# An opening list in another order, and another tile for the kept words' differences

## The chip, the core and the metric

The kernel runs on one core of a Trainium2 chip. Its time is that of the device for one execution, in microseconds, the median of several runs. The core has TensorE (PE; its weight loads are shown apart as PEld), VectorE (DVE), ScalarE (ACT), GpSimd (POOL) and SyncE (SP), which here only issues DMAs. Each works through its own instructions in order and waits on semaphores for the others.

## The reference

Attention over a small memory for 8 batches of 8 heads, 576 tokens and 64 dimensions, then a gated MLP from 512 to 1536 and back on all 4608 tokens. Eps terms and the reshaping are left out.

```python
a = softmax(phi, axis=2)                      # phi: batch, head, 576, 32
k_m = einsum('bhsm,bhsd->bhmd', a, k); v_m = einsum('bhsm,bhsd->bhmd', a, v)
attn = softmax(q @ k_m.T / 8)                 # batch, head, 576, 32
x = (attn @ v_m) with the heads side by side  # 4608 x 512
out = (sigmoid(x @ w_gate) * (x @ w_val)) @ w_out
```

The weights arrive as 64-bit floats. The kernel turns them into 32-bit ones itself.

## The kernel before

Batches are numbered 0 to 7. The inner width of 1536 is cut into 12 stripes f of 128, the tokens of a batch into a first part of 256 (c = 0) and a second of 320 (c = 1). The kernel never forms x: it multiplies the memory's v by each stripe's gate and value weights (the tiles u_hi and u_lo) and multiplies that by the attention (at). Most products are made of three with rounded high and low parts; stripes 0 to 2 of batch 0 are plain ones.

The first twelve steps (stripes 0 to 3 of batches 0, 1 and 2) are not written as loops. OPENING is a list of 401 small tasks, and the kernel emits them in that order. A helper (`step`) makes each engine take its instructions in just the order of the list, so the list sets the order on PE, DVE, ACT and POOL, and that of the DMAs on SP. Some tasks: `phi b`, `kvm b g`, `kvt b`, `q b c` and `words f k r` load (words: the 64-bit weights of stripe f; k = 3 is all of its gate and value weights, 0 and 1 their halves, 2 the output weights); `mag f k` (ACT) and `bits f k` (DVE, two or four goes) convert them; `amax`, `aexp`, `asum` are the softmax of phi; each `mem b n` is the next piece of batch b's memory (transposes, copies, products with k and v); `scores`, `blocks`, `smax`, `sub`, `sexp`, `nsum`, `nmul`, `across`, `upper` and `lower` lead to at (upper and lower are its rounded high part and the rest); `u`, `uhi`, `ulo`; `gate`, `sig`, `mul`, `ghi`, `gleft`, `glo` and `out` are the MLP; `leave` takes a finished accumulator away; and `warm n` is n filling products of 256 columns on an identity matrix, whose result nobody reads.

Behind the list the steps 12 to 35 are loops over the other stripes of batches 0 to 2, with later work put beside them. In six of these steps (KEEP_W, step: pair of stripes) a pair of weight stripes is written back to memory for the batches 3 to 7; for the first 64 rows the second half is written as a difference, which DVE makes in a tile:

```python
for j in range(2):
    t = mb.tile([P, DM], F32, name="row", bufs=4)[:D]
    t = t.rearrange("p (k n) -> p k n", k=NKT)
    nc.vector.tensor_tensor(t, w[:D, j, :, :P], w[:D, j, :, P:], op=ALU.subtract)
    move(kept_k[:D, j, :, P:], t)
```

The tile row has four buffers, which the partial sums of the output use too. The tile e has one; it holds the exponentials of a batch's scores.

Of the kernel before, what the change touches and what calls it, by code (L numbers as in the profile page):

```python
# [49 lines left out]
aexp 0 1; mag 0 1; amax 1; mem 0 2; words 1 3 2; mem 0 4; kvt 0; kvm 0 0; aexp 1 0; asum 0; mem 0 5;  # L50
kvm 0 1; mag 1 3; bits 0 0; mem 0 3; mem 0 1; warm 36; mem 0 11; aexp 1 1; warm 16; mem 0 6; bits 1 3;
phi 2; bits 1 3; asum 1; bits 1 3; mem 0 7; bits 0 1; q 0 0; mem 0 8; mem 0 9; bits 1 3; q 0 1;
mem 1 5; scores 0 0; mem 1 3; bits 0 1; amax 2; aexp 2 0; mem 0 10; mem 1 0; scores 0 1; blocks 0 0;
kvm 1 0; smax 0 0; sub 0 0; u 0 1; blocks 0 1; aexp 2 1; mem 1 4; kvt 1; sexp 0 0; nsum 0 0;
words 2 3 2; mem 1 2; mem 2 1; uhi 0 0 1; u 0 0; uhi 0 1 1; mem 1 1; kvm 1 1; words 1 2 3; mem 2 3;
mem 2 4; uhi 0 0 0; smax 0 1; nmul 0 0; sub 0 1; across 0 0; asum 2; uhi 0 1 0; sexp 0 1; mem 1 11;
mag 2 3; warm 9; gate 0 0 0; gate 0 1 0; sig 0 1 0; mem 2 2; nsum 0 1; sig 0 0 0; bits 2 3; nmul 0 1;
bits 2 3; q 1 0; across 0 1; mem 1 6; mul 0 0 0; mag 1 2; words 0 2 2; bits 2 3; mem 1 7; gate 0 0 1;
bits 2 3; nospread; q 1 1; words 3 2 1; sig 0 0 1; mem 1 8; words 3 3 2; kvm 2 1; mag 0 2; mul 0 1 0;
mul 0 0 1; mem 1 10; mem 1 9; u 0 2; scores 1 0; words 2 2 0; uhi 0 0 2; bits 1 2; bits 0 2; uhi 0 1 2;  # L60
blocks 1 0; gate 0 1 1; sig 0 1 1; ghi 0 0 1; scores 1 1; bits 0 2; mag 3 3; mul 0 1 1; kvm 2 0;
bits 1 2; out 0 0 0; blocks 1 1; bits 3 3; smax 1; gate 0 2 0; kvt 2; mag 2 2; mem 2 0; bits 3 3;
sub 1; gate 0 2 1; sig 0 2 1; sexp 1; words 4 2 2; mem 2 5; gleft 0 0 1; upper 0; out 0 0 1; bits 3 3;
mul 0 2 1; ghi 0 1 1; mem 2 6; bits 3 3; ghi 0 2 1; mem 2 11; sig 0 2 0; out 0 1 0; nsum 1; mem 2 7;
u 0 3; nmul 1; mem 2 8; across 1; uhi 0 0 3; uhi 0 1 3; ulo 0 0 3; out 0 1 1; upper 1; lower 0;
ulo 0 1 3; lower 1; q 2 0; q 2 1; mem 2 10; gate 0 3 1; bits 2 2; mul 0 2 0; gleft 0 2 1; kvt 3;
mag 3 2; gate 0 3 0; sig 0 3 1; sig 0 3 0; mem 2 9; bits 2 2; wohi 2; u 1 0 1; mul 0 3 1; mul 0 3 0;
bits 3 2; out 0 2 0; scores 2 0; out 0 2 1; ghi 0 3 0; uhi 1 0 0 1; uhi 1 1 0 1; scores 2 1; bits 3 2;
ulo 1 1 0 1; u 1 2 3; ghi 0 3 1; ulo 1 0 0 1; gleft 0 3 1; wohi 0; wohi 1; blocks 2 0; gate 1 0 1;
wohi 3; glo 0 3 0; sig 1 0 1; uhi 1 0 2 3; blocks 2 1; gate 1 0 0; gate 1 1 0; sig 1 0 0; glo 0 3 1;  # L70
wolo 3; smax 2; out 0 3 1; mul 1 0 1; sub 2; mul 1 0 0; keep 0; ghi 1 0 1; out 0 3 0; uhi 1 1 2 3;
gleft 0 1 1; wolo 0; wolo 1; words 4 3 0; ulo 1 1 2 3; ulo 1 0 2 3; sig 1 1 0; gate 1 3 0; ghi 1 0 0;
gate 1 1 1; gate 1 2 1; glo 1 0 1; wolo 2; sexp 2; phi 3; glo 1 0 0; gleft 1 0 1; mag 4 2; mul 1 1 0;
sig 1 1 1; leave 0 3; ghi 1 1 0; nsum 2; out 1 0 1; leave 0 1; gate 1 2 0; leave 0 0; mul 1 1 1;
gleft 1 1 1; keep 1; leave 0 2; ghi 1 1 1; nmul 2; glo 1 1 0; kvm 3 0; out 1 0 0; glo 1 1 1; sig 1 2 1;
mag 4 3; bits 4 3; u 2 0 1; sig 1 3 0; sig 1 2 0; u 2 2 3; mul 1 3 0; out 1 1 1; ghi 1 3 0;
uhi 2 0 0 1; bits 4 3; bits 4 3; mul 1 2 1; uhi 2 1 0 1; mul 1 2 0; across 2; gleft 1 2 1; ulo 2 0 0 1;
ulo 2 1 0 1; gate 1 3 1; ghi 1 2 1; upper 2; ghi 1 2 0; glo 1 2 1; bits 4 3; lower 2; out 1 2 1;
glo 1 2 0; sig 1 3 1; mul 1 3 1; bits 4 2; ghi 1 3 1; gleft 1 3 1; bits 4 2; words 5 3 0; uhi 2 0 2 3;
gate 2 0 1; amax 3; sig 2 0 1; wohi 4; ulo 2 0 2 3; mag 5 3; glo 1 3 0; mul 2 0 1; out 1 1 0;  # L80
gate 2 0 0; uhi 2 1 2 3; gleft 2 0 1; bits 5 3; sig 2 0 0; out 1 2 0; aexp 3 1; glo 1 3 1; bits 5 3;
words 6 3 1; bits 5 3; ghi 2 0 1; out 1 3 0; mul 2 0 0; bits 5 3; wolo 4; ulo 2 1 2 3; mag 6 3;
out 1 3 1; words 7 3 0; leave 1 3; glo 2 0 1; gate 2 1 0; ghi 2 0 0; gate 2 1 1; leave 1 0; gate 2 3 1;
glo 2 0 0; sig 2 1 0; gate 2 2 0; sig 2 1 1; mul 2 1 0; sig 2 3 1; ghi 2 1 0; leave 1 1; out 2 0 0;
mul 2 1 1; u 0 4 5; mag 7 3; out 2 0 1; leave 1 2; bits 6 3; glo 2 1 0; again 0; gate 2 3 0;
gate 2 2 1; bits 6 3; sig 2 2 0; keep 2; bits 6 3; gleft 2 1 1; aexp 3 0; bits 7 3; mul 2 2 0;
ghi 2 1 1; ghi 2 2 0; uhi 0 0 4 5; bits 7 3; bits 6 3; mul 2 3 1; sig 2 3 0; glo 2 1 1; ghi 2 3 1;
out 2 1 0; gleft 2 3 1; glo 2 2 0; ulo 0 0 4 5; asum 3; sig 2 2 1; bits 7 3; kvm 3 1; mul 2 3 0;
mul 2 2 1; out 2 2 0; uhi 0 1 4 5; words 5 2 2; ghi 2 3 0; glo 2 3 1; ghi 2 2 1; bits 7 3; words 8 0 1;
ulo 0 1 4 5; glo 2 3 0; glo 2 2 1; words 7 2 0; words 6 2 3; gleft 2 2 1; out 2 1 1  # L90
# [1493 lines left out]
```

## Time and profile before

| | us |
|---|---|
| median of 3 runs (lowest, highest) | 717.69 (717.58, 718.09) |
| the profiled execution | 716.45 |
| its span, first to last instruction | 714.7 |
| PE busy | 705.5 |
| DVE busy | 552.8 |
| ACT busy | 446.3 |

Busy time counts instructions that run, not those that wait. Filling products count as busy for PE. In a timeline a bracket behind a row tells how long the engine had been idle before it and what released it.

### The profile page before, as it was taken

The page shows a single profiled execution, that of the slowest core. Times are in us where ns is not written, and L with a number is a line of the kernel's source. Part 1 is how long each engine was busy: PE and PEld are TensorE (multiplying, and loading weights), DVE is VectorE, ACT ScalarE, POOL GpSimd, SP SyncE. Part 2 cuts the span into 40 slices and gives each one's busy share as a digit, 9 for nine tenths or more (in the row PEclk, how much of TensorE's full clock was granted, in tenths as well). Part 3 has the DMA queues.
Part 4 walks back from the last instruction along what each step waited for, and adds up shares of the span by engine and source line. Part 5 has one row for each costly group of instructions (what it writes and reads, how often), then busy time and mean ns, then how long its engine had stood idle before and what let it go on. Part 6 is the DMA issues. An engine that isn't in the chain of part 4 may idle for free.

```text
span 714.7 us, 14239 instructions
## 1 busy us (share of the span) xinstructions
PE 705.5 (99%) x5517; PEld 579.1 (81%) x5517; DVE 552.8 (77%) x1092; ACT 446.3 (62%) x1033; POOL 27.6 (4%) x55
## 2 busy tenths in 40 slices
PE   8999999999999999999999999999999999999997
PEld 7655898888988888888888888887888788788786
DVE  5898998778787775588887779777797777977663
ACT  4755776543354454467877667875777657686553
POOL 0000100111101110100000000000000000000000
PEclk9999999999999999999999999999999999999999
DMA  8966559878956745642176113652323422151102
GB/s 347 406 261 215 209 193 375 283 276 274 320 183 195 277 140 184 249 129 79 60 260 208 60 60 119 225 186 72 107 73 129 146 88 74 61 176 61 60 1 73
DMA packets 36083, 123.21 MB, mean 172 GB/s; under 512 B 3952, under 2 KB 11376, under 8 KB 28848
## 3 DMA queue, kind: packets, MB, share of 16 engines
...
q10 hardware_dynamic: 160, 0.13, 0.1%
...
## 4 chain that ended last, share of the span: by engine, by line
PE 93%; DMA 3%; ACT 1%; DVE 1%; SPq 1%; issue 0%
PE acc L192 39%; PE pu_t L192 20%; PE c L192 11%; PE a L192 9%; PE b L192 7%; PE d L192 7%; DMA kvm<-in_kvm_dram 2%; DMA words<-in_wo_dram 1%; SPq L178 1%; ACT L162 0%; DVE e L499 0%; DVE e L508 0%; ACT sg L167 0%; DVE mx L506 0%; DVE wg L283 0%
## 5 line engine op out<-in xcount | busy, mean ns | idle before, releaser
L192 PE MATMUL acc<-wo_hi,g_hi 128*128 128x512 f32 x372 | 152.2, 409 | 0.0
L192 PE MATMUL acc<-wo_hi,g_lo 128*128 128x512 f32 x372 | 147.1, 395 | 0.0
L192 PE MATMUL acc<-wo_lo,g_hi 128*128 128x512 f32 x372 | 146.7, 394 | 0.0
L192 PE MATMUL pu_t<-at,u_hi 128*128 128x320 f32 (+1 forms) x560 | 116.7, 305 | 0.0
L192 PEld LDWEIGHTS acc<-wo_hi,g_hi 128*128 128x128 f32 x372 | 69.9, 188 | 37.5 <-ACT c_s L1180 16.8
L192 PEld LDWEIGHTS pu_t<-at,u_hi 128*128 128x128 f32 x560 | 92.1, 188 | 8.5 <-issue 2.1
L192 PEld LDWEIGHTS acc<-wo_hi,g_lo 128*128 128x128 f32 x372 | 69.9, 188 | 16.8 <-DVE g_lo L182 0.3
L192 PE MATMUL pu_t<-at,u_lo 128*128 128x256 f32 (+1 forms) x264 | 77.6, 294 | 0.0
L192 PEld LDWEIGHTS acc<-wo_lo,g_hi 128*128 128x128 f32 x372 | 70.1, 188 | 5.7
L1180 ACT COPY c_p<-c 128x288 f32<-128x288 f32 x60 | 23.9, 398 | 67.3 <-PE c L192 66.6
L167 ACT ACTIVATE sg<-pu_t 128x256 f32<-128x256 f32 (+1 forms) x70 | 28.5, 410 | 49.7 <-PE pu_t L192 45.4
L1184 DVE TENSOR_TENSOR z<-c,c_x 128x288 f32<-128x288 f32 x60 | 27.4, 456 | 34.5 <-PE c L192 31.7
L167 ACT ACTIVATE z<-z 128x288 f32<-128x288 f32 x120 | 48.1, 439 | 8.5 <-DVE z L1184 7.6
L1184 DVE TENSOR_TENSOR z<-a,c_s 128x288 f32<-128x288 f32 x60 | 27.2, 453 | 33.1 <-PE a L192 32.4
L192 PEld LDWEIGHTS pu_t<-at,u_lo 128*128 128x128 f32 x264 | 49.6, 188 | 0.0
L698 DVE TENSOR_TENSOR sg<-pu_t,sg 128x320 f32<-128x320 f32 (+1 forms) x69 | 31.1, 454 | 24.0 <-ACT sg L167 14.2
L708 ACT CAST g_hi<-sg 128x256 fp32r<-128x256 f32 x66 | 26.5, 405 | 36.6 <-DVE sg L698 34.6
L1196 ACT CAST g_hi<-z 128x512 fp32r<-128x512 f32 x60 | 37.3, 622 | 10.4 <-DVE z L1191 10.4
L182 DVE TENSOR_TENSOR g_lo<-z,g_hi 128x512 fp32r<-128x512 f32 x60 | 41.0, 683 | 1.6 <-ACT g_hi L1196 1.6
L1191 DVE TENSOR_TENSOR z<-z 128x288 f32<-128x288 f32 x60 | 27.2, 453 | 6.0 <-ACT z L167 1.1
L192 PE MATMUL c<-ring,vT 64*32 64x512 f32 x232 | 31.4, 601 | 0.0
L192 PE MATMUL a<-ring,vT 64*32 64x512 f32 x232 | 31.4, 601 | 0.0
...
## 6 DMA issues: line engine op xcount, KB each, us to landing
...
at<-at SPq DMA_DIRECT2D x18, 576.0 KB, 7.8
q<-in_qT_dram SPq DMA_DIRECT2D x16, 512.0 KB, 5.0
...
words<-in_wo_dram SPq DMA_DIRECT2D x8, 512.0 KB, 9.6
...
```

Of the source, the lines that this page charges most:

```text
L167: last_act[0] = nc.scalar.activation(*args, **kw)
L178: last_move[queue] = queues[queue].dma_start(dst, src)
L182: return nc.vector.tensor_tensor(lo, x, hi.bitcast(F32), op=ALU.subtract)
L192: last_pe[0] = do(*args, **kw)
L698: last_prod[0] = nc.vector.tensor_tensor(prod, ps[1][:, :n], sg[:, :n], op=ALU.mult)
L708: nc.scalar.copy(hi, prod[:, : 2 * P])
L1180: copy(getattr(self, name), self.c if name == "p5" else self.d)
L1184: nc.vector.tensor_tensor(self.z[:, i], x, y, op=ALU.add)
L1191: nc.vector.tensor_tensor(self.z[:, 2 + i], x, self.z[:, i], op=ALU.mult)
L1196: nc.scalar.copy(self.g[0], self.z[:, 2:4, : 2 * P])
```

## The change

The OPENING list is written anew: the same 401 tasks in another order, with other counts of filling products (46, 40, 3 and 2 in place of 52, 36, 16 and 9). The differences of the kept words are made in the tile e instead of two row tiles, and the pair 4 is kept in step 22 instead of 28.

```diff
 OPENING = """
-words 0 0 0; phi 0; mag 0 0; words 0 1 1; table; phi 1; amax 0; aexp 0 0; bits 0 0; warm 52; mem 0 0;
+phi 1; words 0 0 0; phi 0; table; kvt 0; amax 0; aexp 0 0; words 0 1 1; aexp 0 1; warm 46; mem 0 0;
...
-    KEEP_W = {17: 0, 18: 1, 19: 2, 20: 3, 25: 5, 28: 4}
+    KEEP_W = {17: 0, 18: 1, 19: 2, 20: 3, 22: 4, 25: 5}
...
+            diff = att([P, 2 * S], "e")[:D, : 2 * DM].rearrange("p (f k n) -> p f k n", f=2, k=NKT)
             for j in range(2):
-                t = mb.tile([P, DM], F32, name="row", bufs=4)[:D]
-                t = t.rearrange("p (k n) -> p k n", k=NKT)
+                t = diff[:, j]
                 nc.vector.tensor_tensor(t, w[:D, j, :, :P], w[:D, j, :, P:], op=ALU.subtract)
                 move(kept_k[:D, j, :, P:], t)
```

The first loads on SP's queue stood like this before (the weights' words as words_89, or wg for all of stripe 1; phi of batch 0 as ph, that of batch 1 as in_phiT into wg):

```order
L178 DMA words_89<-in_wgv_dram 128x1024
L178 DMA ph<-in_phiT_dram 128x1152
L178 DMA words_89<-in_wgv_dram 128x1024
L178 DMA wg<-in_phiT_dram 128x1152
L178 DMA wg<-in_wgv_dram 128x2048
L178 DMA kvt<-in_kvt_dram 128x512
```

With the change they stand like this:

```order
L179 DMA wg<-in_phiT_dram 128x1152
L179 DMA words_89<-in_wgv_dram 128x1024
L179 DMA ph<-in_phiT_dram 128x1152
L179 DMA kvt<-in_kvt_dram 128x512
L179 DMA words_89<-in_wgv_dram 128x1024
L179 DMA wg<-in_wgv_dram 128x2048
```

The phi of batch 1 has moved to the front, and that of batch 0 from second to third; the six loads are the same.

The first instructions of ACT, before (wg from words is a magnitude, ph from ph an exponential of batch 0's phi, z from ident loads the table, row from pu_t copies transposes):

```order
L265 ACT_TABLE_LOAD
L265 ACTIVATE wg<-words_89 128x512
L167 ACTIVATE z<-ident 128x1
L167 ACTIVATE ph,z<-ph,nmx 128x576 x2
L265 ACTIVATE wg<-words_89 128x512
L413 COPY row<-pu_t 128x512
```

and with the change:

```order
L168 ACT_TABLE_LOAD
L168 ACTIVATE z<-ident 128x1
L168 ACTIVATE ph,z<-ph,nmx 128x576 x2
L266 ACTIVATE wg<-words_89 128x512 x2
L414 COPY row<-pu_t 128x512
```

The first magnitude has moved behind the two exponentials.

The third place is on DVE, from the conversion of stripe 3 (wg) to lower 0 (at from at, batch 0) and lower 1 (at from q, batch 1); sg and g_hi from pu_t are products of the gate, zs the sums of the scores' exponentials e. Before:

```order
L278 SCALAR_TENSOR_TENSOR wg<-wg 128x1024
L698 TENSOR_TENSOR sg<-pu_t,sg 128x320
L283 SCALAR_TENSOR_TENSOR wg<-wg 128x1024
L521 TENSOR_REDUCE zs<-e 128x36
L522 TENSOR_SCALAR zs<-zs 128x36
L523 RECIPROCAL zs<-zs 128x36
L527 TENSOR_TENSOR e<-e,zs 128x1152
L561 STREAM_TRANSPOSE q<-e 128x1152
L182 TENSOR_TENSOR u_lo<-pu_t,u_hi 128x256
L182 TENSOR_TENSOR at<-at 128x1152
```

With the change:

```order
L279 SCALAR_TENSOR_TENSOR wg<-wg 128x1024
L699 TENSOR_TENSOR sg<-pu_t,sg 128x320 x2
L284 SCALAR_TENSOR_TENSOR wg<-wg 128x1024
L699 TENSOR_TENSOR g_hi<-pu_t,sg 128x256
L522 TENSOR_REDUCE zs<-e 128x36
L523 TENSOR_SCALAR zs<-zs 128x36
L524 RECIPROCAL zs<-zs 128x36
L528 TENSOR_TENSOR e<-e,zs 128x1152
L183 TENSOR_TENSOR u_lo<-pu_t,u_hi 128x256
L562 STREAM_TRANSPOSE q<-e 128x1152
L183 TENSOR_TENSOR at<-at 128x1152
```

The product of gate 0 2 0 (g_hi) has come in ahead of the sums (one of the two sg stood further up before), and u_lo stands ahead of the transpose.

## Rows read from the trace of the kernel before

**Rows 1.** The page, part 1: busy time and share of each engine.
```profile
PE 705.5 (99%) x5517; PEld 579.1 (81%) x5517; DVE 552.8 (77%) x1092; ACT 446.3 (62%) x1033; POOL 27.6 (4%) x55
```

**Rows 2.** Windows: stretch, length, busy PE, PEld, DVE, ACT, POOL, clock, DMA, GB/s.
```profile
0.00:60.00 60.00, 54.70 (x631) 38.51 (x632) 48.05 (x82) 36.62 (x77) 0.69 (x6) 1.00 0.77 302
60.00:700.00 640.00, 640.00 (x4827) 531.36 (x4826) 500.22 (x1003) 404.26 (x945) 26.87 (x49) 1.00 0.47 162
```

**Rows 3.** Timeline of PE in the opening: start, length, instruction, idle before.
```profile
1.36 7.97 PE L192 MATMUL acc<-ident 128*128 128x256 bf16 x52 [1.36 <-POOL ident masks.py:199]
...
10.15 4.09 PE L192 MATMUL acc<-ident 128*128 128x256 bf16 x36
...
18.71 1.08 PE L192 MATMUL pu_t<-kvm,row 128*32 128x128 f32 x32 [0.42 <-DMA kvm<-in_kvm_dram]
...
29.24 1.10 PE L192 MATMUL acc<-at,u_hi 128*128 128x256 f32 x4 [0.35 <-DVE at L564]
```

**Rows 4.** Issue on SP (timeline), and us to landing (DMA view), of two loads.
```profile
1.66 0.43 SPq L178 DMA_DIRECT2D words<-in_wgv_dram  x1
2.13 0.54 SPq L178 DMA_DIRECT2D wg<-in_phiT_dram  x1
...
words<-in_wgv_dram SPq DMA_DIRECT2D x1, 512.0 KB, 6.3
...
wg<-in_phiT_dram SPq DMA_DIRECT2D x1, 576.0 KB, 7.2
```

**Rows 5.** Timeline of DVE and ACT from 6 to 23 us.
```profile
6.67 1.41 DVE L372 TENSOR_REDUCE nmx<-ph 128x1 f32<-128x576 f32 x2 [5.53 <-DMA ph<-in_phiT_dram]
...
8.00 0.42 DVE L271 TENSOR_SCALAR wg<-wg 128x512 f32<-128x512 f32 x1
...
9.04 0.67 ACT L265 ACTIVATE wg<-words 128x512 f32<-128x512 f32 x1
...
22.62 0.45 DVE L499 STREAM_TRANSPOSE e<-acc 128x256 f32<-128x256 f32 x1 [1.16 <-PE pu_t L192]
```

**Rows 6.** Windows in the opening, columns as in rows 2.
```profile
0.00:5.00 5.00, 3.64 (x18) 2.52 (x19) 0.27 (x1) 1.28 (x1) 0.69 (x6) 1.00 0.58 169
5.00:10.00 5.00, 5.00 (x44) 4.43 (x43) 2.73 (x5) 3.15 (x8) 0.00 (x0) 1.00 1.03 424
...
8.00:21.46 13.46, 11.55 (x160) 9.71 (x158) 11.01 (x19) 6.80 (x17) 0.00 (x0) 1.00 1.02 416
22.62:57.63 35.01, 33.00 (x400) 21.11 (x399) 33.09 (x57) 25.15 (x55) 0.00 (x0) 1.00 0.72 284
...
29.24:57.91 28.67, 27.01 (x274) 17.01 (x275) 26.89 (x45) 20.15 (x41) 0.00 (x0) 1.00 0.64 252
```

**Rows 7.** Timeline from 34 to 60 us: DVE's waits, lower 0, PE's load.
```profile
34.15 0.42 DVE L698 TENSOR_TENSOR g_hi<-acc,sg 128x256 f32<-128x256 f32 x1 [0.55 <-ACT sg L167]
...
44.02 0.69 DVE L271 TENSOR_SCALAR wg<-wg 128x1024 f32<-128x1024 f32 x1 [0.18 <-ACT wg L265]
...
50.68 1.35 DVE L521 TENSOR_REDUCE zs<-e 128x36 f32<-128x1152 f32 x1 [0.16 <-ACT e L167]
...
55.94 0.42 DVE L182 TENSOR_TENSOR u_lo<-pu_t,u_hi 128x256 fp32r<-128x256 f32 x1 [0.47 <-ACT u_hi L621]
...
56.28 1.35 DVE L182 TENSOR_TENSOR at<-at 128x1152 fp32r<-128x1152 f32 x1
...
57.91 0.19 PEld L192 LDWEIGHTS pu_t<-at,u_hi 128*128 128x128 f32 x1 [0.24 <-DVE at L182]
...
59.94 0.42 DVE L698 TENSOR_TENSOR g_hi<-pu_t,sg 128x256 f32<-128x256 f32 x1
```

**Rows 8.** Timeline of DVE: the longest wait of a kept words' difference.
```profile
190.73 0.68 DVE L1230 TENSOR_TENSOR row<-wg 64x512 f32<-64x512 f32 x1 [4.16 <-DMA part<-row]
```

**Rows 9.** Timeline at gate 2 0 1: its subtraction on DVE, its first products.
```profile
90.47 1.35 DVE L182 TENSOR_TENSOR at<-q,at 128x1152 fp32r<-128x1152 f32 x1
...
92.39 0.46 PE L192 MATMUL pu_t<-at,u_hi 128*128 128x320 f32 x2
```

More of the change, by code (lines that the diff above doesn't have):

```diff
@@ L48 @@
 OPENING = """
-words 0 0 0; phi 0; mag 0 0; words 0 1 1; table; phi 1; amax 0; aexp 0 0; bits 0 0; warm 52; mem 0 0;
[L50 to L90, printed above, removed]
+phi 1; words 0 0 0; phi 0; table; kvt 0; amax 0; aexp 0 0; words 0 1 1; aexp 0 1; warm 46; mem 0 0;
@@ new lines @@
+words 1 3 2; mag 0 0; mag 0 1; kvm 0 0; mem 0 2; mag 1 3; bits 0 1; bits 0 0; mem 0 4; mem 0 5;
+mem 0 3; amax 1; aexp 1 1; asum 0; mem 0 1; bits 1 3; warm 40; mem 0 11; aexp 1 0; bits 0 1; kvm 0 1;
+bits 1 3; warm 3; mem 0 6; phi 2; mem 0 7; bits 0 0; mem 1 5; bits 1 3; mem 0 8; mem 0 9; q 0 0;
+asum 1; bits 1 3; amax 2; q 0 1; mem 1 3; mem 0 10; aexp 2 0; scores 0 0; blocks 0 0; smax 0 0;
+scores 0 1; aexp 2 1; mem 1 0; mem 2 1; u 0 1; sub 0 0; mem 1 4; sexp 0 0; mem 1 2; uhi 0 0 1; mem 1 1;
@@ new lines @@
+blocks 0 1; mem 2 3; kvm 1 0; kvt 1; u 0 0; uhi 0 1 1; words 2 3 2; uhi 0 0 0; mem 1 11; nsum 0 0;
+words 1 2 3; kvm 1 1; smax 0 1; q 1 0; nmul 0 0; mem 2 4; sub 0 1; uhi 0 1 0; sexp 0 1; mag 2 3;
+across 0 0; warm 2; gate 0 1 0; asum 2; nsum 0 1; gate 0 0 0; words 0 2 2; mag 1 2; bits 2 3;
+nmul 0 1; sig 0 1 0; mem 1 6; bits 2 3; across 0 1; mem 2 2; mem 1 7; sig 0 0 0; words 3 2 1; bits 2 3;
+gate 0 0 1; mul 0 1 0; bits 2 3; mem 1 8; sig 0 0 1; mag 0 2; q 1 1; mul 0 0 0; bits 0 2; u 0 2;
+mem 1 10; bits 1 2; mem 1 9; scores 1 0; nospread; uhi 0 0 2; scores 1 1; words 3 3 2; mul 0 0 1;
@@ new lines @@
+gate 0 1 1; kvm 2 0; sig 0 1 1; uhi 0 1 2; blocks 1 0; mag 3 2; bits 0 2; bits 1 2; ghi 0 0 1; upper 0;
+mag 3 3; blocks 1 1; wohi 1; smax 1; out 0 0 0; gate 0 2 1; words 2 2 0; bits 3 3; sub 1; bits 3 3;
+sig 0 2 1; mem 2 0; gate 0 2 0; gleft 0 0 1; bits 3 3; mul 0 2 1; mem 2 5; kvm 2 1; mul 0 1 1;
+sig 0 2 0; out 0 1 0; bits 3 3; out 0 0 1; mul 0 2 0; kvt 2; sexp 1; nsum 1; u 0 3; gleft 0 1 1;
+ghi 0 1 1; nmul 1; mem 2 6; mem 2 11; ghi 0 2 1; uhi 0 0 3; out 0 1 1; uhi 0 1 3; ulo 0 0 3; across 1;
@@ new lines @@
+mem 2 7; mag 2 2; upper 1; lower 0; mem 2 8; ulo 0 1 3; lower 1; bits 2 2; bits 2 2; mem 2 10;
+bits 3 2; wohi 0; gate 0 3 1; gate 0 3 0; gleft 0 2 1; u 1 0 1; q 2 0; mem 2 9; sig 0 3 1; out 0 2 0;
+sig 0 3 0; scores 2 0; uhi 1 0 0 1; q 2 1; keep 0; out 0 2 1; mul 0 3 1; uhi 1 1 0 1; ulo 1 0 0 1;
+bits 3 2; ulo 1 1 0 1; mul 0 3 0; wohi 3; scores 2 1; u 1 2 3; kvm 3 1; blocks 2 0; gleft 0 3 1;
+ghi 0 3 0; gate 1 0 1; glo 0 3 0; wolo 3; kvm 3 0; ghi 0 3 1; blocks 2 1; glo 0 3 1; gate 1 0 0;
+out 0 3 1; uhi 1 0 2 3; smax 2; words 4 3 0; sig 1 0 1; mul 1 0 1; sub 2; wolo 0; ghi 1 0 1; sig 1 0 0;
@@ new lines @@
+uhi 1 1 2 3; sexp 2; mul 1 0 0; gleft 1 0 1; leave 0 2; gate 1 1 1; wohi 2; gate 1 1 0; ulo 1 0 2 3;
+ulo 1 1 2 3; ghi 1 0 0; nsum 2; glo 1 0 1; gate 1 3 0; sig 1 1 1; glo 1 0 0; sig 1 1 0; wolo 1;
+mul 1 1 0; leave 0 3; sig 1 3 0; out 0 3 0; ghi 1 1 0; out 1 0 1; mul 1 1 1; gate 1 2 1; nmul 2;
+ghi 1 1 1; mag 4 3; gleft 1 1 1; gate 1 2 0; leave 0 0; sig 1 2 1; again 0; bits 4 3; out 1 0 0;
+words 4 2 2; leave 0 1; mag 4 2; glo 1 1 0; glo 1 1 1; across 2; bits 4 3; mul 1 2 1; ghi 1 2 1;
+u 2 0 1; sig 1 2 0; uhi 2 0 0 1; keep 1; u 2 2 3; out 1 1 0; wolo 2; phi 3; mul 1 3 0; mul 1 2 0;
@@ new lines @@
+uhi 2 1 0 1; gate 1 3 1; ghi 1 2 0; bits 4 3; ulo 2 0 0 1; glo 1 2 1; upper 2; ulo 2 1 0 1; bits 4 3;
+out 1 1 1; glo 1 2 0; bits 4 2; sig 1 3 1; lower 2; gleft 1 2 1; out 1 2 1; words 5 3 0; uhi 2 0 2 3;
+mul 1 3 1; ulo 2 0 2 3; ghi 1 3 1; gate 2 0 1; bits 4 2; ghi 1 3 0; sig 2 0 1; glo 1 3 0; gate 2 0 0;
+mag 5 3; glo 1 3 1; sig 2 0 0; mul 2 0 1; amax 3; out 1 2 0; mul 2 0 0; kvt 3; bits 5 3; bits 5 3;
+bits 5 3; uhi 2 1 2 3; gate 2 1 0; ghi 2 0 1; gleft 2 0 1; ghi 2 0 0; out 1 3 1; out 1 3 0; glo 2 0 0;
@@ new lines @@
+words 6 3 1; ulo 2 1 2 3; sig 2 1 0; bits 5 3; gleft 1 3 1; mag 6 3; wohi 4; gate 2 3 1; gate 2 2 0;
+bits 6 3; bits 6 3; gate 2 1 1; sig 2 3 1; wolo 4; mul 2 1 0; leave 1 0; words 7 3 0; leave 1 1;
+mul 2 3 1; keep 2; leave 1 3; ghi 2 1 0; glo 2 0 1; sig 2 2 0; sig 2 1 1; out 2 0 0; glo 2 1 0;
+leave 1 2; bits 6 3; mul 2 1 1; u 0 4 5; mul 2 2 0; aexp 3 0; out 2 1 0; ghi 2 2 0; bits 6 3; mag 7 3;
+gleft 2 1 1; glo 2 2 0; gate 2 3 0; gate 2 2 1; bits 7 3; out 2 0 1; uhi 0 0 4 5; ulo 0 0 4 5;
+ghi 2 1 1; glo 2 1 1; words 5 2 2; aexp 3 1; ghi 2 3 1; sig 2 3 0; bits 7 3; words 6 2 3; asum 3;
@@ L91 @@
+bits 7 3; uhi 0 1 4 5; mul 2 3 0; sig 2 2 1; bits 7 3; ghi 2 3 0; mul 2 2 1; glo 2 3 1; ghi 2 2 1;
+words 7 2 0; out 2 2 0; gleft 2 3 1; glo 2 3 0; ulo 0 1 4 5; words 8 0 1; gleft 2 2 1; glo 2 2 1;
+out 2 1 1
 """
```

## The prediction

> **What bounds the kernel now.** I read the busy times of the page first [rows 1]: TensorE (PE) is busy 705.5 of 714.7 us, the next engine 77%. The table of windows then says where the rest is [rows 2]: from 60 to 700 us PE is busy 640.00 of 640.00 us at a granted clock of 1.00, and 5.3 of its 9.2 idle microseconds lie before 60. So nothing behind 60 us can get shorter by this change; it can only be broken. What the list can move is the time at which the full stretch begins.
>
> The timeline of PE's opening [rows 3] shows waiting in two forms: idle, and filling products, of which 113 run. The first 52 take 7.97 us, the next 36 take 4.09. PE then waits for k and v of batch 0, whose second half (kvm) lets it start at 18.71, and for VectorE's (DVE) transposes of the exponentials, which let the first gate start at 29.24. The reader is to see that the releaser is a DMA first and DVE later, never the filler itself. The windows of DVE [rows 6] carry on: between the first block transposes (22.62) and the end of the subtraction that makes the low part of batch 0's attention (57.63) DVE is busy 33.09 of 35.01 us. That subtraction, lower 0, ends PE's last real wait: the low part's weight load at 57.91 stands with DVE's at as its releaser [rows 7]. So DVE sets the start of the full stretch, and loads and ScalarE (ACT) set when DVE may begin.
>
> **The change, step by step.** Both lists hold the same 401 tasks and differ only in place and in the fillers' counts. Up to gate 0 3 1 (batch 0, stripe 3, second half), the product that waits at 57.91, PE does the same products in both, fillers aside. DVE does the same instructions ahead of lower 0 but for one more, the product of gate 0 2 0. What the change is worth is therefore the shift of that one moment, if nothing behind it breaks.
>
> 1. *Loads.* phi 0 was the second transfer and is now the third, behind phi 1 and the first words. The third transfer landed at 1.66 + 6.3 = 7.96 us and the fourth, 576 KB, at 2.13 + 7.2 = 9.33 [rows 4], so 576 KB take 1.37 us. The first three are now 1664 KB in place of 1600, so phi 0 lands at about 7.96 + 0.15 = 8.1, where DVE's reduction started at 6.67 [rows 5]. The transfers up to the second half of kvm 0 are the same set, so PE's 18.71 stays.
>
> The Trainium skill's page "DMA: Bandwidth & Descriptors" (Specifications) gives about 358 GB/s as HBM's limit for a core. This trace disagrees, with 424 GB/s from 5 to 10 us [rows 6]; by the page's figure 576 KB would take 1.65 us, phi 0 would come 0.3 later, and the sum below would be -0.1 in place of -0.4.
>
> 2. *ACT.* The two magnitudes of stripe 0 now stand behind both exponentials of batch 0. In the trace the reduction starts at 6.67 and the magnitude behind the two exponentials at 9.04, 2.37 later. From a reduction at 8.15 this gives 10.52 for the first magnitude, 0.67 more for the second, and its end at 11.9. DVE's conversions now begin with that second one, so they begin at 11.9 in place of 8.00.
>
> 3. *DVE to the block transposes.* From 8.00 to 21.46 DVE was busy 11.01 us [rows 6], the rest it waited. The same instructions follow in the new order, and their inputs are all there by then (phi 1 lands first of all, the words of stripe 1 some 0.7 later than before, still ahead of their turn). 11.9 + 11.0 = 22.9, against 22.62: **+0.3 us**. Here 3.9 us of lateness go into waits that DVE had anyway.
>
> 4. *The added product.* 0.42 us by its row [rows 7]: **+0.42**, at nothing later on, since it was due there anyway.
>
> 5. *Waits inside 22.62 to 57.63.* Four have a releaser [rows 7]: 0.55 for ACT's sigmoid, 0.18 for ACT's magnitude of stripe 3, 0.16 for an exponential, 0.47 for u_hi. All four have other work ahead of them now: a conversion of 1.2 us stands before the first product, a reduction of 1.3 before stripe 3's first conversion, a product and a conversion before the sum that waited 0.16, and u 0 3 stands ahead of the two memory products of batch 2 instead of behind them. Between 0 and 1.36 us of them go. I take 1.1, nearer the upper end, because each has at least 0.4 us of new cover, and leave 0.25 for waits that the order makes anew.
>
> 6. *Fillers.* 22 fewer, at 4.09 / 36 = 0.114 us. I cost this at nothing: with less filling PE waits idle for the same data. The first 46 end near 8.2, the transposes can start near 9.9; the next 40 end near 15.7, and the 3 behind kvm's first half leave about a microsecond idle before 18.71.
>
> 7. *Kept words' differences.* The subtractions wrote into row tiles and waited for them, 4.16 us at the longest [rows 8], in the stretch in which PE never stops [rows 2]. So to end those waits is worth nothing, and a new wait for the single e tile costs nothing up to about 4.2 us. Each pair now has to wait until the last pair's two 128 KB writes have left; a pair comes every step, and I take 0 for it, with 1 us of PE as its upper bound. The SP queue behind it carries the loads of at for the next turn, which already stood behind such pairs.
>
> Sum: +0.3 + 0.42 - 1.1 = **-0.4 us** at gate 0 3 1, so lower 0 ends near 57.25. PE can be there by then: from its first gate it is busy 27.0 us up to 57.91 [rows 6], and 29.5 + 27.0 = 56.5. The profiled execution took 716.45 us, 1.75 more than its span; the span becomes 714.3 and that execution 716.05. The median of the runs is 717.69, 1.24 above the profiled one, so I forecast **717.3 us**.
>
> **Rivals.**
> *The waits stay or come back elsewhere* (0.23). DVE is then 0.7 late at lower 0: 718.4. For it: only four places are reasoned out here, and ACT, in order too, has more ahead of the second sigmoid. Against it: DVE has 1.9 us of idle to take from.
>
> *The fillers themselves are on the path* (0.14). Then 22 x 0.114 = 2.5 us go, 715.2. For it: the first 52 end after the first exponential is ready. Against it: every filler run is followed by a wait for something else [rows 3].
>
> *The other side: PE's clock falls in a hole that is no longer filled* (0.09). Its place is the hole before 18.71, some 1 us after another of 1.6 us near 9. The first 18 products take 3.64 us or 202 ns each [rows 6], the level of 1.2 GHz, later ones 114, that of 2.4. At the lower level the chain from 18.71 to the first scores, 2.7 us of products, takes 4.8; 0.3 of the 2.1 is hidden, and what follows runs slow until the clock is back: +2 to +4, 719.7 to 721.7. It decides from a fall of 1.5 us in that chain. Against it: the hole of 0.42 us ahead of 18.71 passed at 1.00. The Trainium skill's "TensorE: Matmul & The Clock Gate" (Part 1) calls the throttled state the default, released by activity; no row here shows a fall within the kernel.
>
> *DVE arrives late further on* (0.10). Its place is gate 2 0 1: the subtraction it needs ends at 91.82 and the product starts at 92.39, a lead of 0.57 [rows 9]. With DVE full there, lateness beyond that is PE's; from 2.0 us of it the kernel is slower: 719.2 to 720.5. A wait for the e tile beyond 4.2 us belongs to this case.
>
> **How the numbers follow.** My forecast has 0.44 (its own range 716.9 to 717.8). A change of 0.2%, 1.4 us, is about what a measurement of this kernel can tell from none; 717.3 and 718.4 both lie within it. Within: 0.44 + 0.23 = 0.67. Faster: 0.14. Slower: 0.09 + 0.10 = 0.19. The range leaves out the lower half of the fillers' case and most of the two slow ones: 715.8 to 719.5.
>
> **What would show it.** Right: PE's second kvm product near 18.7 as before; DVE's first conversion near 11.9, its first block transposes near 22.9, lower 0 ending near 57.2, PE full from there to 700 us. Wrong: a first gate beyond 30 us; idle PE between 60 and 120; a clock below 1.00 after 6 us; DVE waits for wgv transfers beyond 4 us with PE idle at once.

## The result and the profile after

The changed kernel took 724.66 us (median of 6 runs, 723.61 to 726.45) beside 717.65 for the kernel before on the same chip: a ratio of 1.0099, 95% interval 1.0083 to 1.0115. It is slower by 1%, and lies above the range of the forecast. The profiled execution took 725.63, with a span of 723.8. One of all the executions reported below, at 857.02 us and a mean granted clock of 0.753, was in a slower state and is left out of its kernel's numbers.

The busy times of the page, which answer to [rows 1]:

```profile
PE 706.0 (98%) x5495; PEld 578.7 (80%) x5495; DVE 552.4 (76%) x1092; ACT 444.2 (61%) x1029; POOL 28.0 (4%) x55
```

No engine has much more to do; the 9.1 us of span are time in which PE waits or runs slowly. The table of windows (columns as in [rows 2]) says where:

```profile
0.00:60.00 60.00, 53.71 (x626) 37.95 (x634) 48.83 (x84) 38.18 (x82) 0.69 (x6) 1.00 0.76 295
60.00:150.00 90.00, 90.00 (x715) 72.56 (x700) 78.19 (x141) 54.85 (x123) 9.23 (x16) 1.00 0.81 296
150.00:200.00 50.00, 42.68 (x260) 36.00 (x260) 34.01 (x72) 16.79 (x43) 7.29 (x13) 0.93 0.80 248
200.00:700.00 500.00, 500.00 (x3793) 415.03 (x3792) 382.37 (x780) 325.70 (x762) 10.82 (x20) 1.00 0.38 130
```

The third row is the one to look at: 7.3 us of idle PE and a clock of 0.93, in a stretch that was full before. The opening, on the contrary, went better than before. These are rows of the timelines of DVE and PE there:

```profile
8.36 1.41 DVE L373 TENSOR_REDUCE nmx<-ph 128x1 f32<-128x576 f32 x2 [7.22 <-DMA ph<-in_phiT_dram]
...
11.99 0.43 DVE L272 TENSOR_SCALAR wg<-wg 128x512 f32<-128x512 f32 x1 [2.21 <-ACT wg L266]
...
17.80 1.08 PE L193 MATMUL pu_t<-kvm,row 128*32 128x128 f32 x32
...
22.78 0.44 DVE L500 STREAM_TRANSPOSE e<-acc 128x256 f32<-128x256 f32 x1
...
29.40 0.89 PE L193 MATMUL acc<-at,u_hi 128*128 128x256 f32 x3 [1.22 <-DVE at L565]
...
55.16 1.32 DVE L183 TENSOR_TENSOR at<-at 128x1152 fp32r<-128x1152 f32 x1
...
56.54 0.42 PE L193 MATMUL pu_t<-at,u_hi 128*128 128x320 f32 x1 [0.84 <-DVE at L183]
...
59.77 1.09 PE L193 MATMUL pu_t<-wg,vT 64*32 64x512 f32 x16
...
66.93 0.56 PE L193 MATMUL pu_t<-at,u_hi 128*128 128x320 f32 x2
```

The low part of batch 0's attention (lower 0) ends at 56.48 in place of 57.63, and gate 1 0 1 starts at 66.93, where it started at 69.15 before. So PE is 2.2 us ahead when it enters the full stretch, and gives back 2.2 + 9.1 = 11.3 us later. The timeline of SP (SPq), DVE and PE from 144 to 194 us shows how:

```profile
144.56 0.90 SPq L179 DMA_DIRECT2D at<-at  x2
145.51 1.44 SPq L179 DMA_DIRECT2D wgv<-wg  x2
147.05 3.50 SPq L179 DMA_DIRECT2D wgv<-e  x2
...
157.24 1.28 DVE L1231 TENSOR_TENSOR e<-wg 64x512 f32<-64x512 f32 x2 [6.96 <-DMA wgv<-e]
...
158.91 0.56 PE L193 MATMUL pu_t<-at,u_hi 128*128 128x320 f32 x2 [1.18 <-DVE sg L699]
...
181.70 3.28 SPq L179 DMA_DIRECT2D wgv<-e  x2
...
190.41 1.29 DVE L1231 TENSOR_TENSOR e<-wg 64x512 f32<-64x512 f32 x2 [6.63 <-DMA wgv<-e]
...
192.23 1.27 DVE L759 TENSOR_TENSOR row<-acc,row 128x512 f32<-128x512 f32 x2
...
193.05 0.77 PE L193 MATMUL acc<-wo_hi,g_hi 128*128 128x512 f32 x1 [4.24 <-DVE row L759]
```

L1231 is the difference of a kept pair. DVE stands still twice, 6.96 and 6.63 us, until the last pair's writes have left the tile e. Behind it stand a gate product (sg) and L759, the adds that free an accumulator; of PE's 7.3 idle us it waits 1.2 for the first and 6.1 for the adds. Pair 0's writes were issued only at 147.05, since SP has the loads of at (2 x 576 KB) and the pair's other writes (768 KB) ahead of them, and landed near 157. The hole before 193.05 has a second price. Windows of one microsecond show it:

```profile
190.00:191.00 1.00, 0.00 (x0) 0.00 (x0) 0.58 (x1) 0.00 (x0) 0.00 (x0) 0.97 0.88 254
191.00:192.00 1.00, 0.00 (x0) 0.00 (x0) 1.00 (x3) 0.00 (x0) 0.00 (x0) 0.50 0.14 39
...
196.00:197.00 1.00, 1.00 (x6) 1.00 (x6) 1.00 (x3) 0.00 (x0) 0.61 (x2) 0.50 0.45 76
197.00:198.00 1.00, 1.00 (x8) 1.00 (x7) 1.00 (x4) 0.55 (x2) 0.99 (x3) 0.62 0.80 258
198.00:199.00 1.00, 1.00 (x7) 0.82 (x6) 1.00 (x3) 0.67 (x2) 0.23 (x1) 1.00 1.00 395
```

The granted clock (third number from the end) is 0.50, the level of 1.2 GHz, from 190.9 to 197.8 us, that is from 2.1 us after PE ran out of work up to 4.7 us after it has work again. What this costs is read from the starts of the same two products, first in the kernel before, then with the change (the first of these two is the row at 193.05 above):

```profile
186.50 0.39 PE L192 MATMUL acc<-wo_hi,g_hi 128*128 128x512 f32 x1
...
189.31 0.39 PE L192 MATMUL acc<-wo_hi,g_hi 128*128 128x512 f32 x1
```

```profile
198.07 0.39 PE L193 MATMUL acc<-wo_hi,g_hi 128*128 128x512 f32 x1
```

From one to the other it takes 5.02 us in place of 2.81, so the low clock costs 2.2. At the first of them PE, 2.2 ahead before, is 6.55 behind: 8.75 lost, of which 7.3 are idle time. The other 1.4 lie inside busy time: products overlap (0.39 us long, 0.23 apart), so each of the five gaps is 0.16 longer between starts than its idle time says, and the first products behind a gap run slower. Together that is 11.0 of the 11.3.

What the prediction did not look up is where the differences now stand. Behind the list DVE's order is set by a scheduler (the program is built with `schedule_with_timeline_sim=True`), and the tile changes it: pair 0's difference runs at 140.14 here, and at 162.46 in the run list_step below, which differs from the changed kernel in the tile alone. That the scheduler moved it because it reckons the tile e free early is likely, but not shown. With the tile e the differences of the pairs 1 and 4 stand right ahead of what a turn's end needs. This is DVE's order around pair 1 with the change (sg<-pu_t,sg are gate products, row<-acc,row the adds):

```text
L183 TENSOR_TENSOR u_lo<-pu_t,u_hi 128x512 x4
L1231 TENSOR_TENSOR e<-wg 64x512 x2
L699 TENSOR_TENSOR sg<-pu_t,sg 128x256
L272 TENSOR_SCALAR wg<-wg 128x512
L699 TENSOR_TENSOR sg<-pu_t,sg 128x320
L275 TENSOR_SCALAR wg<-wg 128x512
L759 TENSOR_TENSOR row<-acc_1658,row 128x512
```

In list_step, as in the kernel before, even pair 0's differences stand behind all four adds of this turn, the last of which starts at 157.98. These are its differences of pair 0, and the one with the longest wait:

```profile
162.46 1.30 DVE L1231 TENSOR_TENSOR row<-wg 64x512 f32<-64x512 f32 x2 [1.21 <-DMA part<-row]
...
189.08 0.68 DVE L1231 TENSOR_TENSOR row<-wg 64x512 f32<-64x512 f32 x1 [4.22 <-DMA part<-row]
```

### The profile page after: what moved, and what is told of

It is laid out like the page before. It is cut to its first block, busy times and chain, and to the rows that moved or that the text cites. A ratio compares the mean times of both kernels' runs of the same rounds, so it can differ in the third digit from the quotient of the medians.

```text
span 723.8 us, 14194 instructions
## 1 busy us (share of the span) xinstructions
PE 706.0 (98%) x5495; PEld 578.7 (80%) x5495; DVE 552.4 (76%) x1092; ACT 444.2 (61%) x1029; POOL 28.0 (4%) x55
## 4 chain that ended last, share of the span: by engine, by line
PE 88%; DVE 7%; DMA 3%; issue 1%; ACT 1%; SPq 0%; DVEq 0%; ACTq 0%
PE acc L193 37%; PE pu_t L193 18%; PE c L193 11%; PE a L193 9%; PE b L193 7%; PE d L193 7%; DMA wgv<-e 2%; DMA ph<-in_phiT_dram 1%; DVE wg L284 1%; DVE wg L279 1%; DVE nmx L373 0%; DVE wg L272 0%; DVE e L500 0%; DVE e L1231 0%; DVE wg L275 0%
```

## Experiments

Ratios are to the kernel before, run on the same chip beside each set; their 95% intervals stand behind them.

**Which part of the change it is.** Four kernels take the parts one by one: the new list alone; the tile and the step without the list; the list with the row tiles and the new step; the list with the tile e and the old step.

```diff
 # list_alone: OPENING of the change, the rest of before
 # tile_and_step: OPENING of before, the rest of the change
 # list_step: the change, but
-            diff = att([P, 2 * S], "e")[:D, : 2 * DM].rearrange("p (f k n) -> p f k n", f=2, k=NKT)
-                t = diff[:, j]
+                t = mb.tile([P, DM], F32, name="row", bufs=4)[:D]
+                t = t.rearrange("p (k n) -> p k n", k=NKT)
 # list_tile: the change, but
-    KEEP_W = {17: 0, 18: 1, 19: 2, 20: 3, 22: 4, 25: 5}
+    KEEP_W = {17: 0, 18: 1, 19: 2, 20: 3, 25: 5, 28: 4}
```

> The new opening list alone, with the row tiles and the steps of before. Theory T (the differences in the single tile e make VectorE wait for their own writes, and the list by itself is a gain): TensorE is 2.1 us ahead of the kernel before from 66.9 us on, as it is in the changed kernel up to 148, and keeps that lead to the end: about 715.5 us, ratio 0.997. Rival R1 (the new list itself leaves the steps 17 to 22 worse off): about 724.7, ratio 1.010. Rival R2 (keeping pair 4 in step 22, right behind pair 3, crowds the writes): 715.5 here as well.

> The opening list of before, with the differences in the tile e and pair 4 in step 22. T and R2: the loss of some 9 to 11 us between 150 and 200 us is all there without the lead of 2.1, so 726.7 to 728.7, ratio 1.013 to 1.015, with a hole of 4 to 5 us on TensorE near 190 and a granted clock near 0.6 behind it. R1: 717.7, ratio 1.000.

> The changed kernel with the differences back in row tiles; pair 4 stays in step 22. T: no wait for wgv transfers that TensorE feels, about 715.5 us, ratio 0.997. R2: the hole near 190 us stays, 720 to 724.7.

> The changed kernel with the differences in the tile e, but pair 4 back in step 28. T: the wait of pair 1 for pair 0's writes (6.96 us, 4.4 us of idle TensorE near 157 to 166) stays; that of pair 4 for pair 3's (6.63 us, 4.5 us of idle and 6.8 us at half clock) goes, since ten steps lie between them: 715.5 + 4.4 = about 719.9, ratio 1.003. R2: all of the loss goes, 715.5.

Measured: the list alone 715.24 us, 0.997 (0.9958 to 0.9983); the tile and the step 726.93, 1.0133 (1.0103 to 1.0163); list and step with row tiles 714.80, 0.9967 (0.9954 to 0.998); list and tile with the old step 725.26, 1.0104 (1.0067 to 1.014), its four runs from 722.4 to 727.4. So the list is a gain of 0.3%, the tile e a loss of 1.3%, and the step changes nothing with row tiles: R1 and R2 fall. Theory T held on three of four. It missed on list_tile, where I had the wait of pair 4 go with nothing in its place. The one before 190 us did go, but in the profiled execution, the fastest of the four, PE lost 1.4 us near 214 and 2.6 near 246 instead (2.4 of it waiting for DVE's block transposes, which write into the tile e). The windows of list and step with row tiles have no idle PE, though DVE's longest wait there was 4.22 us:

```profile
150.00:200.00 50.00, 50.00 (x346) 42.90 (x344) 39.63 (x85) 20.43 (x54) 7.05 (x13) 1.00 0.84 268
200.00:700.00 500.00, 500.00 (x3780) 416.50 (x3773) 383.05 (x781) 326.93 (x765) 10.86 (x20) 1.00 0.37 128
```

**What the wait is made of.** The tile and the step stay; the writes, the order or the room change.

```diff
 # tile_first: the differences' writes ahead of the pair's others
-            move(kept_k[D:], w[D:])
-            move(kept_k[:D, :, :, :P], w[:D, :, :, :P])
...
                 move(kept_k[:D, j, :, P:], t)
+            move(kept_k[D:], w[D:])
+            move(kept_k[:D, :, :, :P], w[:D, :, :, :P])
 # adds_first: differences ordered behind the adds emitted so far
+                    if last_leave[0] is not None:
+                        order.enter_context(tc.issue_after(last_leave[0].ins))
                     nc.vector.tensor_tensor(t, w[:D, j, :, :P], w[:D, j, :, P:], op=ALU.subtract)
```

> The changed kernel, with the two writes of a pair's differences put on SP's queue ahead of the pair's other 768 KB. In the changed kernel those two writes of pair 0 were issued from 147.05 us, behind two loads of at (144.56) and two writes from wg (145.51), and VectorE waited for them until 157.24. Theory Q1 (the wait is long because the writes stand behind the other 768 KB): they are issued at 145.5, land 4.5 to 7 us later, VectorE waits 0 to 2 us instead of 7, likewise 1.5 to 3 instead of 6.6 near 190: 715.5 to 717.5 us. Rival Q2 (the sixteen DMA engines are full there, share 0.99, so the place in the queue gives little): waits of 5 us and more, 721 to 725.

> The changed kernel, with each difference ordered behind the last accumulator add that the program has emitted by then, so that no add which frees an accumulator stands behind a waiting difference of the pairs 1 and 4. The tile e stays single. Theory O1 (the waits cost time because the adds stand behind them): VectorE still waits 6 us and more for the tile, but TensorE idles at most 1 us in all between 150 and 200: 715.5 to 717.5 us. Rival O2 (a VectorE that stands still for 7 us stops TensorE whatever is behind it, through the products of the gate): 719 to 724.

Measured: 720.49 us, 1.0045 (1.0028 to 1.0063), and 721.13, 1.0052 (1.0034 to 1.0071). Rival Q2 is the nearer (the waits were 4.89 and 4.90), though the time is a little better than it had, and Q1 falls. With the small writes first, the timelines of SP and DVE read:

```profile
145.90 1.37 SPq L179 DMA_DIRECT2D wgv<-e  x2
...
154.94 1.28 DVE L1229 TENSOR_TENSOR e<-wg 64x512 f32<-64x512 f32 x2 [4.89 <-DMA wgv<-e]
```

Two writes of 128 KB, issued at 145.90 right behind the loads of at, were gone only near 154.9, 9.0 us later (the median for such a write is 4.5 in the changed kernel). Their place in the queue gave 2 us of the 7. With the adds first O1 falls and the time lies in O2's range: the waits of the pairs 1 and 4 went, and pair 3 waited 4.25 us at 175.92, now ahead of the low parts u_lo, and PE with it:

```profile
175.92 1.29 DVE L1235 TENSOR_TENSOR e<-wg 64x512 f32<-64x512 f32 x2 [4.25 <-DMA wgv<-e]
...
179.86 0.79 PE L193 MATMUL pu_t<-at,u_hi 128*128 128x256 f32 x2 [4.44 <-DVE u_lo L183]
```

So it is not the adds that matter but whatever PE wants next.

```diff
 # tile_early: KEEP_W = {16: 0, 17: 1, 18: 2, 19: 3, 22: 4, 25: 5}, and again(...), the loads of at, behind the pair's writes
-        if i in returns:
-            again(returns[i])
         if i in KEEP_W:
...
+        if i in returns:
+            again(returns[i])
 # two_halves: one tile e for two pairs
+            if k % 2 == 0:
+                both = att([P, 2 * S], "e")[:, : 2 * DM].rearrange("p (f k n) -> p f k n", f=2, k=NKT)
+            diff = both[k % 2 * D : k % 2 * D + D]
 # mixed: even pairs in the tile e, odd pairs in row tiles
 # tile_pool: nc.gpsimd.tensor_tensor for nc.vector.tensor_tensor
```

> The changed kernel with the tile e, but the pairs 0 to 3 kept one step earlier (16 to 19) and each pair's writes put on SP's queue ahead of the loads of at for the next turn. Theory S (the two long waits are those for the pairs 0 and 3 alone, whose writes stand on SP's queue, and then in the DMA engines, behind 1152 KB of at: issued at 147.05 and 181.70 us in the changed kernel, landed 8.7 to 10.2 later): pair 0's writes now land before 150, pair 3's before 175, no wait of VectorE for wgv is above 3 us, TensorE idles less than 1 us: 715.0 to 717.0 us. Rival B (one tile for six pairs is too little room wherever the writes stand): waits of 5 us and more, 720 to 725.

> The changed kernel with room for two pairs in the tile e (the even pair in the rows 0 to 63, the odd one in 64 to 127). Theory S: the room doesn't help much, since pair 2 now waits for the pairs 0 and 1 and pair 4 for the pairs 2 and 3, and pair 3's writes still stand behind the loads of at: waits of 5 us and more near 155 and 185, 719 to 725. Rival B: with twice the room the waits go, 715.0 to 717.0 us.

> The changed kernel with the even pairs' differences in the tile e and the odd ones' in row tiles, so that each tile has two steps in place of one. Theory S: pair 2 stands on VectorE where pair 1 stood and waits for pair 0's writes as that did, 6 to 7 us near 157, while pair 4 waits for pair 2's, which stand behind no load of at, so the wait near 190 and the low clock go: about 719.9 us, ratio 1.003. Rival B: twice the room ends both waits, 715.0 to 716.5.

> The changed kernel with the differences made by GpSimd instead of VectorE, in the same tile e at the same steps; the tile still waits for its own writes. Theory D (what costs is that VectorE, which takes its instructions in order, stands still): VectorE no longer waits for wgv, TensorE idles less than 1 us between 60 and 700, 715.0 to 717.0 us. Rival L (the writes and loads that crowd the DMA engines cost TensorE its time whoever waits, or GpSimd's own loads of words queue up behind the waiting difference and come late): 719 to 725.

Measured: tile_early 719.64 us, 1.0026 (1.001 to 1.0042), its runs from 716.8 to 723.1 (without the one named above); two_halves 720.38, 1.0037 (1.0023 to 1.0051); mixed 725.67, 1.0118 (1.0099 to 1.0137); tile_pool 725.15, 1.0103 (1.0079 to 1.0127).

With pair 0's and pair 3's writes ahead of the loads of at, no wait is above 3.4 us, nearly as theory S had it (3). But pair 0's writes left the tile at 152, not before 150, PE idled 2.3 us in place of less than 1, and the time missed its 717: a short wait still costs when it stands right ahead of the low parts. Rows of DVE and PE in tile_early:

```profile
152.14 1.28 DVE L1229 TENSOR_TENSOR e<-wg 64x512 f32<-64x512 f32 x2 [2.26 <-DMA wgv<-e]
...
154.08 0.56 PE L193 MATMUL pu_t<-at,u_hi 128*128 128x320 f32 x2 [1.52 <-DVE u_lo L183]
```

Twice the room (two_halves) shortens the two waits to 3.73 and 3.90 us and does not end them; the time lies in S's range, though S had the waits at 5 and more. The two halves are one tile and come free together (pair 2's wait ended at 160.44, behind pair 1's writes, issued at 152.75), so this is not a second buffer taken in turn. The Trainium skill's "Trainium Kernel Development and Optimization" (Best Practices) says to double-buffer so that transfers overlap with work; here the room for two pairs gave back 0.6 of the 1.3% and the four row tiles all of it. In mixed, pair 2 took pair 1's place on DVE and waited 6.16 us, as S had it; but pair 4 waited too, 4.28 us, because pair 2's writes (made ready at 157.6) stood on SP behind pair 1's, whose row tile came late, and were issued at 172.83; behind that wait PE idled 5.69 us for the low parts. Rival B, for which both waits were to go, falls. So a write can be held up on SP by any transfer ahead of it, not only by the loads of at.

The run with the differences on GpSimd shows what the standing still is worth by itself. Its windows, and its timeline of POOL and PE:

```profile
150.00:200.00 50.00, 50.00 (x346) 42.75 (x345) 38.83 (x73) 19.19 (x49) 18.43 (x21) 1.00 0.77 237
200.00:250.00 50.00, 44.69 (x338) 38.44 (x331) 33.66 (x67) 19.50 (x48) 7.47 (x13) 0.93 0.70 241
```

```profile
191.19 2.99 POOL L1231 TENSOR_TENSOR e<-wg 64x512 f32<-64x512 f32 x2 [16.38 <-DMA wgv<-e]
...
199.69 1.07 POOL L179 DMA_DIRECT2D q<-in_wo_dram  x2
...
207.28 0.79 PE L193 MATMUL pu_t<-at,u_hi 128*128 128x256 f32 x2 [5.31 <-DVE u_lo L183]
```

While DVE is free of the wait, PE is full from 150 to 200 us with the same transfers in flight: theory D, for that stretch, though not for its time. But POOL now stands still for 16.38 us, the output weights that it loads (q<-in_wo_dram) come late, ScalarE waits 8.17 us for them, and PE idles 5.3 us at 207 (the second half of rival L). The wait goes to whoever stands behind it in its engine's order.

**The clock.** Thirty products are put into the hole before 193 us.

```diff
 # hole_filled, in gate_half
             i = 0
+            if (b, f, c, w) == (2, 5, 1, 1):
+                for _ in range(30):
+                    matmul(pt[:, :n], terms[0][0][:, 0, ws], terms[0][1][:, 0, cs], start=True, stop=True)
```

> The changed kernel, with 30 products of 320 columns (147 ns each, 4.4 us) ahead of the last gate product before the hole of 4.5 us near 188.5 us; they write into that gate's own bank, which is then started anew. Theory C1 (the granted clock of about 0.5 from 190.9 to 197.8 us comes of the hole, and costs 6.8 / 2 = 3.4 us beside the idle time): TensorE is busy through the hole, the clock stays at 1.00 there and the time falls by about 3.4: 721.3. Rival C2 (the clock falls for another reason, such as the transfers in flight): 724.7 with the low clock still there. Rival C3 (the filling delays the gate, and VectorE with it): above 725.

Measured: 723.34 us, 1.0077 (1.0059 to 1.0095). Its windows, and its timeline of DVE and PE:

```profile
190.00:195.00 5.00, 5.00 (x35) 4.74 (x34) 4.96 (x12) 0.41 (x1) 2.74 (x5) 1.00 0.68 191
195.00:200.00 5.00, 5.00 (x30) 4.48 (x29) 4.32 (x10) 2.07 (x6) 0.59 (x2) 1.00 1.02 371
```

```profile
187.77 1.29 DVE L1234 TENSOR_TENSOR e<-wg 64x512 f32<-64x512 f32 x2 [4.96 <-DMA wgv<-e]
...
192.07 0.39 PE L193 MATMUL acc<-wo_hi,g_hi 128*128 128x512 f32 x1
...
194.88 0.39 PE L193 MATMUL acc<-wo_hi,g_hi 128*128 128x512 f32 x1
```

The clock stays at 1.00 with the transfers in flight, so it was the hole that lowered it, and C2 falls. The two products that were 5.02 us apart at the low level are 2.81 apart here, so it cost 2.2. My price of 3.4 was too high: it counted all 6.8 us at the low level, of which PE idled 2.1 anyway. Between the ratios lie 0.0022, 1.6 us, with intervals that overlap. C3's range was missed, but the delay that it names was there: DVE's wait ended 2.64 earlier in this execution (187.77 beside 190.41), and PE came to the first of the two products only 0.98 earlier, since the filling and the gate behind it lasted until then. The Trainium skill's "TensorE: Matmul & The Clock Gate" (Terms) multiplies the whole throttled time by the share of pulses that are lost, which is my 3.4; where the low level begins within a wait, the rows give less.

**Where the gain of the list comes from.** The fillers are put back to their old counts in list_step; and in the kernel before one or two tasks are moved.

```diff
 # fillers_back: list_step with warm 52, 36, 16, 9 for 46, 40, 3, 2
 # u_ahead: the list of before, with
-gate 0 3 0; sig 0 3 1; sig 0 3 0; mem 2 9; bits 2 2; wohi 2; u 1 0 1; mul 0 3 1;
+gate 0 3 0; mem 2 9; bits 2 2; wohi 2; u 1 0 1; sig 0 3 1; sig 0 3 0; mul 0 3 1;
 # vt_ahead: the list of before, with
-gate 0 3 0; sig 0 3 1; sig 0 3 0; mem 2 9; bits 2 2; wohi 2; u 1 0 1; mul 0 3 1;
+gate 0 3 0; mem 2 9; sig 0 3 1; sig 0 3 0; bits 2 2; wohi 2; u 1 0 1; mul 0 3 1;
```

> The new list with row tiles and pair 4 in step 22 (ratio 0.9967 in its own run), with the filling products in the old counts: 52, 36, 16 and 9 in place of 46, 40, 3 and 2. Theory F1 (as the prediction's sixth step has it, fillers lie in waits and cost nothing): ratio 0.9967 again, 715.1 us beside 717.5. Rival F2 (they are on the path, and dropping 22 of them at 0.114 us is where the lead of 2.1 us comes from): up to 2.5 us more, ratio 1.000, 717.5.

> The kernel before with one edit in its list: the sigmoids of gate 0 3 stand behind u 1 0 1 on ScalarE instead of ahead of it, nothing else moves. In the kernel before the 16 products of u 1 0 1 (61.18 us) take 1.89 us, because their third weight load waits 0.67 for ScalarE's copy of vT behind a sigmoid; with the new list they take 1.09. Theory V (that copy is the second half of the new list's gain): 1.1 us for the 16 products, the stretch behind them 0.7 to 0.8 earlier, ratio 0.999. Rival W (the late sigmoids hold up the products behind, so the gain is lost): ratio 1.000 to 1.002, with a wait for VectorE's products within 5 us.

> The kernel before with only ScalarE's copy of vT put ahead of the two sigmoids of gate 0 3; the cast of wo_hi, which waited for VectorE and held the sigmoids up in the run with u 1 0 1 ahead, stays behind them. Theory V (the copy of vT behind a sigmoid was TensorE's last wait, and its end is the second part of the new list's gain): the 16 products of u 1 0 1 take 1.1 us instead of 1.89, gate 1 0 1 starts 0.7 to 0.8 earlier than 69.15, ratio 0.999. Rival W (the products wait for a bank that a sigmoid must have read, whatever the copy does): u 1 0 1 takes 1.6 us or more, gate 1 0 1 starts less than 0.3 earlier, ratio 1.000.

Measured: 714.93 us, 0.9959 (0.9945 to 0.9974), so the fillers are free (F1); u_ahead 718.05, 1.0011 (1.0 to 1.0023); vt_ahead 716.77, 0.9988 (0.9975 to 1.0), which by its time alone is not told from no gain. The kernel before has a wait inside the 16 products of u 1 0 1, which the row of PE (1.89 us, in one piece) hides and that of its weight loads shows:

```profile
61.18 1.89 PE L192 MATMUL pu_t<-wg,vT 64*32 64x512 f32 x16
...
61.57 0.37 ACT L456 COPY vT<-pu_t 128x256 f32<-128x256 f32 x1
...
61.99 0.18 PEld L192 LDWEIGHTS pu_t<-wg,vT 64*32 64x32 f32 x14 [0.67 <-ACT vT L456]
```

With the copy of vT alone moved ahead of the sigmoids, the same products take 1.09 us, as with the new list:

```profile
58.51 0.86 PE L192 MATMUL pu_t<-at,u_hi 128*128 128x320 f32 x2
...
62.18 1.09 PE L192 MATMUL pu_t<-wg,vT 64*32 64x512 f32 x16
...
69.34 0.55 PE L192 MATMUL pu_t<-at,u_hi 128*128 128x320 f32 x2
```

From the gate product to gate 1 0 1 it is 69.34 - 58.51 = 10.83 us, in the kernel before 69.15 - 57.51 = 11.64: 0.8 less, as theory V had it. In u_ahead the sigmoids had also gone behind a cast that waited 3.22 us for DVE, and PE waited 0.51 for one of them: rival W for that edit, which moved more than it was to test.

The version that beats both kernels is the new list with row tiles, in whichever step pair 4 is kept and with either count of fillers: 0.997, 0.9967 and 0.9959, which their intervals do not tell apart.

## Why the prediction was wrong

**Loads, ACT, DVE to the block transposes** held: the reduction of phi 0 at 8.36 (8.15 forecast), the first conversion at 11.99 (11.9), the block transposes at 22.78 (22.9), the first gate at 29.40 (29.5). The second kvm product came at 17.80, where I had it stay at 18.71.

**The added product and the waits inside** held in mechanism and were mis-sized. I took 1.1 us of the waits' 1.36; from 22.78 to the end of lower 0 DVE is now busy 33.14 of 33.70 us, idle 0.56 in place of 1.92, so 1.36 went. And of the 0.42 for the added product the busy time shows 0.05 (33.09 before). The sum at lower 0's end is -1.15 in place of -0.4.

**"Lower 0 ends PE's last real wait"** was false. The wait for vT in u 1 0 1 is another, worth 0.8 us; the row of 640.00 busy microseconds hid it, because products count as busy while they are in flight. Behind lower 0, which ends 1.15 earlier, the products of u 1 0 1 start 61.18 - 59.77 = 1.41 earlier and take 0.80 less: the 2.2 that PE is ahead. With this alone the kernel would have been faster by 0.3%, as list_alone is: without the tile, 717.3 would still have been nearly 2 us too high.

**The fillers** cost nothing where they stand, as said. The rival that PE's clock falls in a hole which they no longer fill did occur: in the opening of 8 of the 11 profiled executions of the new list with the new counts (not in that of the changed kernel), and in none of the five, of either list, with the old counts. In that of list_step the first 46 end at 7.99, PE idles until 10.21, and from 11.16 the clock is at the low level for 3.4 us:

```profile
11.00:12.00 1.00, 1.00 (x6) 0.94 (x7) 0.00 (x0) 1.00 (x3) 0.00 (x0) 0.58 1.01 426
12.00:14.00 2.00, 2.00 (x11) 1.45 (x10) 1.87 (x5) 1.65 (x4) 0.00 (x0) 0.50 1.03 434
14.00:15.00 1.00, 1.00 (x9) 0.77 (x8) 1.00 (x2) 0.48 (x2) 0.00 (x0) 0.72 0.98 410
```

Its first gate came at 29.89 instead of 29.40: 0.5 us, not the 2 to 4 that I had priced. With the old counts back (fillers_back) the clock stayed at 1.00, so the 22 fillers left out may have been worth such half a microsecond; the ratios, 0.9967 and 0.9959, do not tell. The price took its low level from the 202 ns of the first products, a stretch whose clock column reads 1.00; the changed kernel bears it out, where products of 256 columns started 0.21 us apart at 0.50.

**The kept words' differences** are the step that failed: "a new wait for the single e tile costs nothing up to about 4.2 us. Each pair now has to wait until the last pair's two 128 KB writes have left; a pair comes every step, and I take 0 for it, with 1 us of PE as its upper bound." The wait was seen, and its size was never worked out. I took 4.2 us from the longest wait of the kernel before and asked neither how long a write takes from VectorE's difference to its landing (with the change 141.42 to 157.24, 15.8 us: 5.6 until SP issued it, 10.2 from there, with 1152 KB of at and 768 KB of the pair's other words ahead of it) nor what stands behind the difference on DVE. Both could be estimated ahead: the first from SP's timeline, the second from the order of the changed program. The last rival held the right mechanism ("A wait for the e tile beyond 4.2 us belongs to this case") with a chance of 0.10 and 719.2 to 720.5 us; the two waits were 6.96 and 6.63 us and cost 11.3, the fall of the clock included, which I had looked for in the opening alone. The last sign of being wrong, waits for wgv beyond 4 us with PE idle at once, is the one that came. Nor is 4.2 us a bound: 4.22 cost nothing in list_step, while 2.26 ahead of the low parts cost 1.52 in tile_early.

What is not settled: why two 128 KB writes need 9.0 us behind the loads of at even when they are the next in the queue. The DMA engines are busy there, 0.99 of the time from 150 to 155 us in the changed kernel, but no run took the loads away.
